# Attention scores on eight array tiles, token reads on two row tiles

## The chip, the cores and the metric

The kernel runs on one core of a Trainium2 chip. The core has a matrix engine (TensorE, PE in the profile; its weight loads are shown as PEld), VectorE (DVE), ScalarE (ACT), GpSimd (POOL) and SyncE (SP, which only issues transfers here). The metric is the device time of one execution in microseconds; lower is better.

## What is computed

Three layers follow one another. The change touches the first and the format in which it hands over.

```python
# attention: B=8, H=8, S=512 tokens, Ns=32 state rows, D=64 a head
scores = scale * x @ state.T              # per batch and head: 512 x 32
a      = softmax(scores, axis=-1)
xread  = a @ state                        # 512 x 64 (reads of the tokens)
scores2 = scale * state @ x.T             # 32 x 512, the same products
sread  = softmax(scores2, axis=-1) @ x    # 32 x 64 (reads of the state)
x = concat([xread, sread], axis=2)        # 4352 tokens of 512, heads side by side
# first expert network: top 1 of 8 experts by cosine logits / tau
out[mask_e] = gate * (relu(x[mask_e] @ w1[e]) @ w2[e])     # 512 -> 1024 -> 512
# second network: h = x @ w_in;  y = (h * clip(h + 3, 0, 6) / 6) @ w_out   # 512 -> 2048 -> 512
```

## The kernel before

**How it is ordered.** All instructions are placed by hand-written planning code (`Sched`, from line 49). Each step is an `op` with a function that emits its instructions, a cost for each engine that may do it, a priority in time, the steps it depends on, and buffers that it takes and gives back (`Ring`, `Hold`). At build time `Sched.run` simulates the engines and emits the steps in the order that the simulation finds. Each engine then runs its own instructions in exactly that order; waits on semaphores are added by the framework. A changed cost, dependency or ring therefore reorders the whole program. The number of buffers of each kind stands in `RG`: four PSUM tiles of two banks in the attention (`ps`), one of each of most intermediate results, and six row buffers (`row`) of which incoming rows may hold five (`rin`).

**The attention, one batch** (`batch`, line 776; steps named `o_...`). The tokens of a batch are loaded for each head (`o_x`, line 489; the first two batches in two halves, `o_xs` and `o_xt`). TensorE transposes pairs of heads (`o_X`, line 529), which puts 2 x 64 channels on the 128 partitions, ScalarE or VectorE copies them to `xT` (`o_Xc`). For each half v of the heads, `o_sc` (line 541) multiplies them with `stT`, the transposed state: for a pair of heads a stationary tile of 128 x 64 with the 32 state rows of one head in its upper left and of the other in its lower right, zeros elsewhere. So a score product contracts over 128 partitions, half of them against zeros, and writes 64 PSUM partitions. VectorE scales the scores to SBUF with a running minimum (`o_scs`). Two softmaxes follow. For the state's reads: exponentials on ScalarE (`o_e2`), transposes (`o_a2`), a copy, and products on column tiles of 128 x 32 (`o_sr`, line 621). For the tokens' reads: transposes (`o_sT`), minimum, subtraction, exponentials, sum, reciprocal, product (`o_rm` to `o_nm`, the last on GpSimd or VectorE), transposes (`o_aT`), a copy (`o_ah`), and for each of four row blocks r the reads (`o_xr`, line 657): for each half g of the heads one product of 128 x 128 with `sd`, the masked state, 264 columns wide. `sd` is made by GpSimd (`o_sd`, line 515); it also carries 8 columns that give each token's expert logits (from `gq`, the state times the expert embeddings). The reads are copied from PSUM to `xr` (`o_xrc`), the logits summed over g (`o_lga` on GpSimd, `o_lg` on VectorE for the last two batches) and `xr` stored to DRAM (`xd`).

**A row of `xd`** has 512 values in four quarters, each with two pieces of 64 values and two partial logits: W = 528 floats, 2112 bytes.

**After the attention** comes the routing (lines 880 to 1120: ranks, slots, indices), then the expert network, which gathers rows of `xd` (`gather` and `parts`, lines 1271 and 1276), rearranges them (`perm`, `blocks`, `bh`, `bl`), multiplies (lines 1412, 1453 and 1515) and stores its outputs (`yt` to `ysd`); interleaved with it the second network reads `ysd` in blocks (`yl`), multiplies (lines 1621 and 1656) and scatters to the output (`yo`). Its weights are converted along the way by ScalarE, VectorE and GpSimd (`convert`, `Conv`; lines 295 to 326), the first ones during the attention. Gathered rows, expert outputs, blocks, final outputs and late conversions share the row buffers.

Of the kernel before, what the change touches and what calls it, by code (L numbers as in the profile page):

```python
# [154 lines left out]
def kernel(  # L155
# [27 lines left out]
    W = DM + 2 * E  # L183
# [32 lines left out]
    def quarters(t, g):  # L216

        v = t.rearrange("p (q g w) -> p g q w", q=4, g=2)[:, g]
        return v[:, :, 0:64].rearrange("p q (i a) -> p q i a", i=2), v[:, :, 64:66]
# [29 lines left out]
    RG = {n: Ring(k) for n, k in dict(  # L249
        ps=4, ax=NAX, xT=NXT, scs=NSC, e2=NE2, e1=NE1, a2=NA2, ah=NAH, xr=NXR, sd=2, sx=1, xs=1, acr=2,  # L250
        m=2, raw=NRAW, w=NW, wraw=NRAW, craw=2, cv=2, cvl=2, gx4=1, gp=2, gx=NGX, gps=6, row=NROW, rin=5, x=1, hx=NHX,
# [130 lines left out]
    SP.dma_start(em, emb)  # L382
# [37 lines left out]

    bmask = one.tile([128, 4], F32, name="bmask")
# [38 lines left out]
    def o_stc(b0, b1, hp):  # L460
        pv = flat(V["st", b0])[:, 0:(b1 - b0) * 256].rearrange("p (u hp n) -> p u hp n", hp=2, n=NS)
        o = stT[64 * hp:64 * hp + 64, b0:b1, :, NS * hp:NS * hp + NS]
        (DVE.tensor_copy if hp else ACT.copy)(o.rearrange("p b u n -> p (b u) n"), pv[64 * hp:64 * hp + 64, :, hp, :])

    def o_gq(b0, b1):
        p = V["gq", b0] = ps("gq_ps")
        for b in range(b0, b1):
            for u in range(4):
                k = (b - b0) * 2 + u // 2
                PE.matmul(p[64 * (u % 2):64 * (u % 2) + 64, 0, k * E:(k + 1) * E],  # L470
                          stT[:, b, u, :], enT[:, u, :], start=True, stop=True)

    def o_gqc(b0, b1):
        ACT.copy(gq[:, b0:b1], V["gq", b0][:, 0, 0:(b1 - b0) * 2 * E].rearrange("p (b g e) -> p b g e", g=2, e=E))
# [14 lines left out]
    def o_x(b, u):  # L489
        if u == 0:  # L490
            V["x", b] = big("xb")[:, 0:R * DM].rearrange("p (r h d) -> p r h d", r=R, h=H)
        SP.dma_start(V["x", b][:, :, u, :], x[b, u].rearrange("(p r) d -> p r d", r=R))
# [8 lines left out]
    def o_xt(e, b, v):  # L501
# [3 lines left out]
        for k in range(2):  # L505
            rs = slice(2 * k, 2 * k + 2)
            {"A": ACT.copy, "D": DVE.tensor_copy, "P": POOL.tensor_copy}[e](
                V["x", b][:, rs, hs, :], V["xs", b][:, hs, rs, :].rearrange("p h r d -> p r h d"))
# [6 lines left out]
    def o_sd(b):  # L515
        t = V["sd", b] = ap2.tile([128, 2, W // 2], F32, tag="sd", name="sd")
        for g in range(2):
            v = t[:, g].rearrange("p (h q w) -> p h q w", h=2, q=2)
            for h in range(2):
                POOL.tensor_tensor(  # L520
                    v[:, h, :, 0:64].rearrange("p q (i a) -> p q i a", i=2),
                    stk[:, b, g, :].rearrange("p (q a) -> p q a", q=2).unsqueeze(2).to_broadcast([128, 2, 2, 32]),
                    bmask.rearrange("p (i h) -> p h i", i=2)[:, h].unsqueeze(1).unsqueeze(3).to_broadcast([128, 2, 2, 32]),
                    op=ALU.mult)
        POOL.tensor_copy(t.rearrange("p g (q w) -> p g q w", q=4)[:, :, :, 64:66],
# [15 lines left out]
    def o_sc(b, v, r0, r1):  # L541
        if (v, r0) == (0, 0):
            V["sc", b] = ps("sc_ps")
        t, k = V["xT", b, v], slice(r0 * 128, r1 * 128)
        for w in range(2):
            PE.matmul(V["sc", b][64 * w:64 * w + 64, v, k], stT[:, b, 2 * v + w, :], t[:, w, k], start=True, stop=True)
# [74 lines left out]
    def o_sr(b):  # L621
        xb, a2 = V.pop(("x", b)), V.pop(("a2", b))
        p = V["sr", b] = ps("sr_ps")
        for g in range(2):
            for r in range(R):
                for h in range(4):
                    PE.matmul(p[NS * h:NS * h + NS, 0, g * D:(g + 1) * D],
                              a2[:, r, (4 * g + h) * NS:(4 * g + h + 1) * NS], xb[:, r, 4 * g + h, :],
                              start=r == 0, stop=r == R - 1)

    def o_sx(b):
        p, r2 = V.pop(("sr", b)), V.pop(("s2", b))
        if b % 4 == 0:
            V["sx", b // 4] = ap1.tile([128, 2, 4, D], F32, tag="sx", name="sx")
# [1240 lines left out]
```

## Time and profile before

| | us |
|---|---|
| median of 3 runs | 1436.18 (1435.46 to 1437.13) |
| the profiled execution | 1427.65 |
| its span, first to last instruction | 1426.0 |
| TensorE busy | 1340.8 (94%) |
| VectorE busy | 867.1 (61%) |
| ScalarE busy | 606.6 (43%) |
| GpSimd busy | 414.7 (29%) |
| mean granted TensorE clock | 0.972 of full |

The profile is one execution, 8.5 us shorter than the median of the timed runs. Times of instructions come from it; busy time is the union of an engine's instructions. Consecutive instructions of an engine overlap a little in the records, so a duration can be some 0.1 us longer than the pace. Matmul ends are modelled. A product of two 32-bit operands shows as two TensorE instructions, a transpose as one.

### The profile page before, as it was taken

The numbers are of one execution on the slowest core, as the hardware profiler recorded it, in microseconds if no ns is written. First come the engines' busy times: TensorE is split into PE (matmuls) and PEld (weight loads), VectorE is DVE, ScalarE is ACT, GpSimd is POOL, SyncE is SP. The second block draws the span as 40 slices with busy tenths as digits, with TensorE's granted clock in tenths as the row PEclk, the third lists the DMA queues.
The fourth block names the chain that finished last, engine by engine and source line by source line (L and its number), as shares of the span: only waits on it lengthen the run. The fifth ranks groups of instructions, "written<-read, shape, count | busy, mean of one in ns | idle before, by whom it ended". The sixth has DMA issues, their size and how long they took to land. (4 is left out here: it accounts for less than half of the span.)

```text
span 1426.0 us, 24825 instructions
## 1 busy us (share of the span) xinstructions
PE 1340.8 (94%) x8912; PEld 1184.8 (83%) x8912; DVE 867.1 (61%) x2037; ACT 606.6 (43%) x1313; POOL 414.7 (29%) x441
## 2 busy tenths in 40 slices
PE   7985797968999999999999999999999999999997
PEld 5764776867789899888989899998989999899996
DVE  6777865777775455545555456777766676434432
ACT  4875635556534333332424333433434444333332
POOL 4333545312343241323223223333334311100000
PEclk9998789997999999999999999999999999999999
DMA  6654346556663243333333334554545544101000
GB/s 163 180 175 165 106 133 201 156 157 205 185 186 113 90 120 112 98 104 91 126 90 120 96 105 125 165 148 141 172 144 163 161 141 141 54 16 31 15 16 15
DMA packets 151761, 175.59 MB, mean 123 GB/s; under 512 B 43784, under 2 KB 116488, under 8 KB 150608
## 3 DMA queue, kind: packets, MB, share of 16 engines
q1 hardware_dynamic: 128544, 121.19, 28.5%
q0 software_dynamic: 12336, 35.99, 8.2%
q10 hardware_dynamic: 10752, 16.78, 3.6%
q8 instruction: 71, 1.16, 0.4%
q14 instruction: 58, 0.48, 0.1%
HBM read 146.09 MB, written 27.82 MB: 122 GB/s over the span
## 5 line engine op out<-in xcount | busy, mean ns | idle before, releaser
L1621 PE MATMUL u_ps<-yh,wih 128*128 128x256 f32 x1088 | 308.3, 283 | 17.0 <-DVE gl L1635 6.9
L1621 PE MATMUL u_ps<-yw,wih 128*128 128x256 f32 x1088 | 307.9, 283 | 0.1
L1621 PE MATMUL u_ps<-yh,wil 128*128 128x256 f32 x1088 | 307.3, 282 | 0.0
L1625 ACT ACTIVATE r<-u_ps,three 128x256 f32<-128x256 f32 x272 | 129.0, 474 | 353.0 <-PE u_ps L1621 350.1
L1628 DVE SCALAR_TENSOR_TENSOR u_ps<-r,u_ps 128x256 f32<-128x256 f32 x272 | 116.5, 428 | 228.9 <-ACT r L1625 224.5
L1621 PEld LDWEIGHTS u_ps<-yh,wih 128*128 128x128 f32 x1088 | 207.9, 191 | 27.3 <-ACT yh L295 6.9
L1656 PE MATMUL o<-woh,gh 128*128 128x512 f32 x544 | 216.5, 398 | 3.0 <-DVE yo L1670 1.8
L1656 PE MATMUL o<-wol,gh 128*128 128x512 f32 x544 | 215.6, 396 | 0.0
L1621 PEld LDWEIGHTS u_ps<-yw,wih 128*128 128x128 f32 x1088 | 207.4, 191 | 8.4 <-DVE yw L1600 0.4
L1656 PE MATMUL o<-woh,gl 128*128 128x512 f32 x544 | 214.3, 394 | 0.0
L1621 PEld LDWEIGHTS u_ps<-yh,wil 128*128 128x128 f32 x1088 | 208.0, 191 | 0.0
L1251 DVE TENSOR_TENSOR wl<-raw,wh 128x512 fp32r<-128x512 f32 x277 | 194.0, 711 | 8.5 <-ACT wh L1248 3.8
L1632 ACT CAST gh<-u_ps 128x256 fp32r<-128x256 f32 x272 | 101.2, 372 | 205.1 <-PE o L1656 170.2
L1515 PE MATMUL y_ps<-wh,hx 128*128 128x512 f32 x512 | 184.8, 397 | 0.0
L1635 DVE TENSOR_TENSOR gl<-u_ps,gh 128x256 fp32r<-128x256 f32 x272 | 114.9, 422 | 110.7 <-ACT gh L1632 110.1
L1251 POOL TENSOR_TENSOR wl<-raw,wh 128x512 fp32r<-128x512 f32 x75 | 103.9, 1385 | 229.1 <-DVE wh L1248 121.7
L1279 POOL DMA_INDIRECT xq<-xd,qidx x128 | 130.2, 1017 | 80.6 <-DVE xt L1332 39.1
L1248 DVE CAST wh<-raw 128x512 fp32r<-128x512 f32 x229 | 102.0, 448 | 65.5 <-DMA raw<-in_moe_w_dram 24.4
L1412 PE MATMUL h_ps<-xt,wh 128*128 128x256 f32 x704 | 136.7, 283 | 1.8 <-DVE wh L1248 1.8
L1675 POOL DMA_INDIRECT out_dram<-yo,ix x34 | 37.0, 1090 | 317.8 <-DVE yo L1670 219.3
L1656 PEld LDWEIGHTS o<-woh,gl 128*128 128x128 f32 x544 | 102.1, 188 | 24.9
L1656 PEld LDWEIGHTS o<-woh,gh 128*128 128x128 f32 x544 | 102.2, 188 | 19.6 <-DVE yo L1670 2.2
(296 smaller groups left out, 2234.0 us busy)
## 6 DMA issues: line engine op xcount, KB each, us to landing
raw<-in_moe_w_dram SPq DMA_DIRECT2D x176, 512.0 KB, 3.9
yl<-ysd SPq DMA_DIRECT2D x136, 64.0 KB, 3.0
xd<-xr SPq DMA_DIRECT2D x8, 1056.0 KB, 5.0
ysd<-yt POOLq DMA_DIRECT2D x32, 256.5 KB, 3.3
xb<-in_x_dram SPq DMA_DIRECT2D x48, 128.0 KB, 3.1
yw<-in_moe_w_out_dram ACTq DMA_DIRECT2D x9, 512.0 KB, 3.5
cv_raw<-in_moe_w_in_dram ACTq DMA_DIRECT2D x8, 512.0 KB, 4.8
yh<-in_moe_w_in_dram ACTq DMA_DIRECT2D x8, 512.0 KB, 5.3
```

The lines of the kernel that those rows point to most:

```text
L1248: copy[e](pc["hi"], box["t"][:, j, :])
L1251: eng[e].tensor_tensor(pc["lo"], box["t"][:, j, :], f32(pc["hi"]), op=ALU.subtract)
L1279: POOL.indirect_dma_start(q[:, j * QW:(j + 1) * QW], None, xd_q, index(qidx[:, j, s:s + 1]))
L1412: PE.matmul(out(f), pc[w][:, (2 * c + f) * 128:(2 * c + f + 1) * 128], u.xt[a][:, 2 * j + c, 256 * hf:256 * hf + 256], start=new and c == ...
L1515: PE.matmul(u.y[i], u.ht[t][:, a, lo + 128 * i:lo + 128 * i + 128], pc[w], start=c == 0 and k == 0, stop=c == KF - 1 and k == 2)
L1621: PE.matmul(p, w, y[:, k, :], start=k == 0 and j == 0, stop=k == KD - 1 and j == 2)
L1625: ACT.activation(q["r"], q["p"], AF.Relu, bias=pool["three"][:, 0:1], scale=unit_i)
L1628: DVE.scalar_tensor_tensor(q["p"], q["r"], 6.0, q["p"], op0=ALU.min, op1=ALU.mult)
L1632: ACT.copy(q["h"], q["p"])
L1635: DVE.tensor_tensor(q["l"], q["p"], f32(q["h"]), op=ALU.subtract)
L1656: PE.matmul(o["o"][a], g[:, a * 128:(a + 1) * 128], w, start=m == 0 and j == 0, stop=m == KFF - 1 and j == 2)
L1675: POOL.indirect_dma_start(out, bass.IndirectOffsetOnAxis(ap=o["ix"][:, a:a + 1], axis=0), box["t"], None)
```

## The change

**Scores.** `stT` becomes a dense tile of 32 columns a pair (no zeros, no clearing); heads u and u + 4 are paired instead of 2u and 2u + 1, so that the tokens and outputs of a batch stand in another order of heads. A score product contracts over 64 partitions and writes 32: eight products a batch, on two row halves (each its own PSUM bank) by four column quarters, in one step that waits for both halves' copies. `o_gq` does the same for the logits.

**Reads of the tokens.** The masked state `sd` has half the columns, and each of four products per row block contracts over 64 partitions and writes 136 columns; the two row halves write different banks. A row now has four pieces of 32 values with two partial logits each in every quarter: W = 544, and each logit is a sum of four parts.

**Planner.** `o_sc` costs 0.1 + 0.00085 n and `o_xr` 0.5 where it was 0.9; the copies `X0c`, `a2c` and `x2c` may go to either engine. Row buffers go from six to five, those for incoming rows from five to four. The rest follows the new format. The diff, cut:

```diff
-    W = DM + 2 * E
+    W = DM + 4 * E
-    NRAW, NW, NROW, NGX = 2, 3, 6, 4
+    NRAW, NW, NROW, NGX = 2, 3, 5, 4
-... row=NROW, rin=5, ...
+... row=NROW, rin=4, ...
-    SP.dma_start(em, emb)
+    for i in range(2):
+        SP.dma_start(em.rearrange("e (u i d) -> e i u d", i=2, u=4)[:, i], emb.rearrange("e (i u d) -> e i u d", i=2, u=4)[:, i])
+    DVE.tensor_tensor(bmask[:, 0:2], bmask[:, 0:2], bmask[:, 2:4], op=ALU.add)
-    stT = one.tile([128, B, 4, 2 * NS], F32, name="stT")
-    DVE.memset(stT[:, 0:1], 0.0)
-    POOL.memset(stT[:, 1:B], 0.0)
+    stT = one.tile([128, B, 4, NS], F32, name="stT")
     def o_gq(b0, b1):
-                PE.matmul(p[64 * (u % 2):64 * (u % 2) + 64, 0, k * E:(k + 1) * E],
-                          stT[:, b, u, :], enT[:, u, :], start=True, stop=True)
+                for g in range(2):
+                    PE.matmul(p[NS * u:NS * u + NS, g, k * E:(k + 1) * E], stT[64 * g:64 * g + 64, b, u, :],
+                              enT[64 * g:64 * g + 64, u, :], start=True, stop=True)
     def o_x(b, u):
-        SP.dma_start(V["x", b][:, :, u, :], ...)
+        SP.dma_start(V["x", b][:, :, 2 * (u % 4) + u // 4, :], ...)
     def o_sd(b):
-            for h in range(2):
-                POOL.tensor_tensor(... 2 x 2 x 32 values, bmask of 4 ...)
+            POOL.tensor_tensor(... 2 x 2 x 32 values, bmask[:, 0:2] ...)
-    def o_sc(b, v, r0, r1):
-        for w in range(2):
-            PE.matmul(V["sc", b][64 * w:64 * w + 64, v, k], stT[:, b, 2 * v + w, :], t[:, w, k], start=True, stop=True)
+    def o_sc(b, r0, r1):
+        for u in range(4):
+            for g in range(2):
+                PE.matmul(V["sc", b][NS * u:NS * u + NS, g, k], stT[64 * g:64 * g + 64, b, u, :],
+                          V["xT", b, u // 2][64 * g:64 * g + 64, u % 2, k], start=True, stop=True)
     def o_xr(b, r):
-            PE.matmul(p[:, g, 0:256 + E], V["ah", b][:, g, r * 128:(r + 1) * 128], V["sd", b][:, g, :], start=True, stop=True)
+            for i in range(2):
+                h = slice(64 * i, 64 * i + 64)
+                PE.matmul(p[:, i, g * QW:(g + 1) * QW], V["ah", b][h, g, r * 128:(r + 1) * 128], V["sd", b][h, g, :],
+                          start=True, stop=True)
     def o_lg(b, r):
-        DVE.tensor_tensor(t, t, p[:, 1], op=ALU.add)
+        for k in range(1, 4):
+            DVE.tensor_tensor(t, t, p[:, k // 2, k % 2], op=ALU.add)
     def o_lga(xr, j, n):
-        POOL.tensor_tensor(lg[...], l[:, :, 0], l[:, :, 1], op=ALU.add)
+        POOL.tensor_tensor(t, l[:, :, 0:2], l[:, :, 2:4], op=ALU.add)
+        POOL.tensor_tensor(lg[...], t[:, :, 0], t[:, :, 1], op=ALU.add)
-        X0c='A', X1c='*', ah='*', nm='P', a2c='A', x0c='*', x1c='*', x2c='A', x3c='*', q1='A')
+        X0c='*', X1c='*', ah='*', nm='P', a2c='*', x0c='*', x1c='*', x2c='*', x3c='*', q1='A')
     def batch(b, t, last):
-                a = do(f"X{v}", o_X, {"T": 0.00085 * n}, xl_[b][4 * v:4 * v + 4], [hX], args=(v, *rr))
+                a = do(f"X{v}", o_X, {"T": 0.00085 * n}, [x_ for i in range(2) for x_ in xl_[b][4 * i + 2 * v:4 * i + 2 * v + 2]], [hX],
+                       args=(v, *rr))
-                f = do(f"c{v}", o_sc, {"T": 0.00086 * n}, [c, *st_ready[b]], ...)
+            f = do("c1", o_sc, {"T": 0.1 + 0.00085 * n}, [*cs_, *st_ready[b]], ...)
-            a = do("xr", o_xr, {"T": 0.9}, deps[r], ...)
+            a = do("xr", o_xr, {"T": 0.5}, deps[r], ...)
```

## Rows read from the trace of the kernel before

**Rows 1.** Busy time by stretch: length, each engine (instructions), clock, DMA share, GB/s

```profile
18.00:104.00 86.00, 80.74 (x966) 60.71 (x965) 63.47 (x138) 65.75 (x111) 28.56 (x46) 1.00 0.59 170
104.00:138.00 34.00, 21.68 (x186) 17.10 (x184) 25.11 (x77) 18.97 (x32) 9.63 (x12) 0.89 0.40 140
...
235.00:400.00 165.00, 136.20 (x796) 119.39 (x796) 117.89 (x261) 92.06 (x189) 50.88 (x51) 0.92 0.61 180
400.00:1426.00 1026.00, 1010.60 (x6455) 909.86 (x6453) 575.72 (x1329) 377.33 (x866) 259.73 (x251) 1.00 0.35 107
```

**Rows 2.** Waits of TensorE, 18 to 104 us: total us, times, longest

```profile
PE sc_ps L546 <- ACT e L566: 1.0, 2, 0.5
```

**Rows 3.** Busy time from 40 to 100 us, columns as in rows 1

```profile
40.00:100.00 60.00, 57.13 (x594) 43.81 (x590) 45.05 (x94) 47.45 (x79) 25.03 (x40) 1.00 0.67 199
```

**Rows 4.** Timeline (start, length, engine, line, operation): scores of batches 2 and 7

```profile
39.37 1.92 PE L546 MATMUL sc_ps<-xT,stT 128*64 128x512 f32 x8
...
97.10 1.52 PE L546 MATMUL sc_ps<-xT,stT 128*64 128x256 f32 x12
```

**Rows 5.** Timeline of one batch: scores of one half, reads, transposes' loads

```profile
50.37 1.08 PE L546 MATMUL sc_ps<-xT,stT 128*64 128x512 f32 x4
...
51.58 3.83 PE L663 MATMUL xr_ps<-sd,ah 128*128 128x264 f32 x16
...
58.59 0.91 PEld L533 LDWEIGHTS xT_ps<-ident,xb 128*128 128x128 f32 x8
```

**Rows 6.** Groups by line, 18 to 131 us: count, busy us, mean ns, idle before

```profile
L666 ACT COPY xr<-xr_ps 128x528 f32<-128x528 f32 x26 | 15.6, 599 | 16.4 <-PE xr_ps L663 11.9 <-issue 4.6
...
L326 POOL TENSOR_TENSOR wil<-cv_m,wih 128x512 fp32r<-128x512 f32 x6 | 7.7, 1279 | 14.1 <-ACT wih L323 14.1
L627 PEld LDWEIGHTS sr_ps<-xb,a 128*32 128x32 f32 x512 | 7.5, 110 | 3.0 <-ACT a L619 1.4 <-DVE e L594 0.8 <-ACT xr L666 0.3
...
L309 DVE SCALAR_TENSOR_TENSOR cv_raw<-cv_raw 128x512 int32<-128x512 int32 x6 | 4.0, 674 | 0.0
```

**Rows 7.** Timeline of the start

```profile
0.87 0.39 SPq L382 DMA_DIRECT2D em<-in_moe_expert_emb_dram  x1
...
1.98 1.59 POOL L429 MEMSET stT<- 128x1792 f32 x1
...
2.77 0.85 DVE L414 TENSOR_SCALAR oi<-orow 128x34 int32<-128x34 int32 x1
...
3.90 0.15 DVE L418 TENSOR_SCALAR oi<-pi 128x1 int32<-128x1 int32 x1
...
6.98 5.22 DVE L441 TENSOR_SCALAR em<-em,ss 8x512 f32<-8x512 f32 x1
```

**Rows 8.** Last batch's token loads, its first transposes, and the loads' landing

```profile
75.92 5.90 SPq L492 DMA_DIRECT2D xb<-in_x_dram  x8
...
86.54 1.04 PE L533 MATMUL xT_ps<-ident,xb 128*128 128x128 f32 x8
...
xb<-in_x_dram SPq DMA_DIRECT2D x48, 128.0 KB, 3.1
```

**Rows 9.** Timeline of the attention's end, and the first gather

```profile
127.05 2.05 PE L663 MATMUL xr_ps<-sd,ah 128*128 128x264 f32 x8 [0.74 <-ACT ah L655]
...
129.97 0.16 DVE L674 TENSOR_TENSOR lg<-lg,xr_ps 128x8 f32<-128x8 f32 x1
...
139.32 1.43 POOL L1273 DMA_INDIRECT xg<-xd,gidx  x1 [13.69 <-DVE cv_raw L309]
```

**Rows 10.** Busy time 160 to 170 us, columns as in rows 1

```profile
160.00:170.00 10.00, 10.00 (x86) 10.00 (x85) 9.65 (x20) 5.64 (x11) 4.18 (x3) 1.00 0.47 151
```

**Rows 11.** Waits, 235 to 400 us, columns as in rows 2

```profile
PE u_ps L1621 <- DVE yt L1539: 4.9, 1, 4.9
...
POOL xg L1273 <- DMA ysd<-yt: 3.9, 2, 3.1
...
ACT yt L1535 <- DMA ysd<-yt: 3.3, 1, 3.3
```

More of the change, by code (lines that the diff above doesn't have):

```diff
@@ L212, with quarters @@
     xd_q = xd.rearrange("t (q w) -> (t q) w", q=4)
-    def quarters(t, g):
-        v = t.rearrange("p (q g w) -> p g q w", q=4, g=2)[:, g]
-        return v[:, :, 0:64].rearrange("p q (i a) -> p q i a", i=2), v[:, :, 64:66]
+    def quarters(t):
+        v = t.rearrange("p (q c w) -> p c q w", q=4, c=4)
+        return v[:, :, :, 0:32], v[:, :, :, 32:34]
     ctx.enter_context(tc.manual_schedule())
@@ L633, in o_sx @@
         if b % 4 == 0:
-            V["sx", b // 4] = ap1.tile([128, 2, 4, D], F32, tag="sx", name="sx")
+            V["sx", b // 4] = ap1.tile([128, 4, 2, D], F32, tag="sx", name="sx")
         sx = V["sx", b // 4]
@@ L638, in o_sx @@
             DVE.tensor_tensor(
-                sx[q:q + NS, :, h, :],
+                sx[q:q + NS, h, :, :],
                 p[NS * h:NS * h + NS, 0, 0:2 * D].rearrange("p (g k) -> p g k", g=2),
@@ L695, in o_q2 @@
         p, t = V["sxp", q], V["sxT", q]
-        for g in range(2):
-            for i in range(2):
-                PE.matmul(p[:, 1, g * 16:g * 16 + E], t[:, 2 * g + i, :], enT[:, 2 * g + i, :],
-                          start=i == 0, stop=i == 1)
+        for c in range(KD):
+            PE.matmul(p[:, 1, c * E:(c + 1) * E], t[:, c, :], enT[:, c, :], start=True, stop=True)
     def o_q3(q):
         xr = V["xrs", q] = ap1.tile([128, 1, W], F32, tag="xrs", name="xrs")
-        for g in range(2):
-            ACT.copy(quarters(xr[:, 0], g)[0],
-                     V["sx", q][:, g].rearrange("p h d -> p (h d)").rearrange("p (i q a) -> p q i a", i=2, q=4))
+        for c in range(KD):
+            ACT.copy(quarters(xr[:, 0])[0][:, c].rearrange("p (h k) a -> p h k a", h=2),
+                     V["sx", q][:, c % 2 * 2:c % 2 * 2 + 2, c // 2].rearrange("p h (k a) -> p h k a", k=2))
     def o_q4(q):
-        for g in range(2):
-            DVE.tensor_copy(quarters(V["xrs", q][:, 0], g)[1],
-                            V["sxp", q][:, 1, g * 16:g * 16 + E].rearrange("p (q i) -> p q i", q=4))
+        DVE.tensor_copy(quarters(V["xrs", q][:, 0])[1],
+                        V["sxp", q][:, 1, 0:KD * E].rearrange("p (c q e) -> p c q e", c=4, q=4))
     PB, P0 = 9.31, 9.54
@@ L1298, in perm @@
             o["q"] = pool["g_p"].tile([128, KD, 128], F32, tag="xp", name="xp")
-            for g in range(2):
-                copy[e](o["q"][:, 2 * g:2 * g + 2, :].rearrange("p i (q a) -> p q i a", q=4), quarters(o["t"], g)[0])
+            copy[e](o["q"].rearrange("p c (q a) -> p c q a", q=4), quarters(o["t"])[0])
         def tr():
```

79 lines of the change are left out of this document (40 added, 39 removed).

## The prediction

> **What bounds the kernel now.** I read the busy time of the engines by stretch first [rows 1]. Up to 104 us, in the attention, TensorE works 80.74 of 86 us. Behind it comes a short stretch to 138 us in which every engine has gaps (the end of the attention and the routing), then the lead of the expert network, from 235 to 400 us a stretch where TensorE is busy 83% of the time, and from 400 us on 98% at full clock. The last kilomicrosecond is therefore bound by TensorE's own work, which the change does not touch: what is won or lost before 400 us simply moves it.
>
> The waits of TensorE in the attention come next [rows 2]: the largest total is 1.0 us, so it runs out of work almost nowhere and is the bound there. The question is how far the others are behind it. Between 40 and 100 us it is busy 57.13 of 60 us, ScalarE 47.45, VectorE 45.05, GpSimd 25.03 [rows 3]. The scores of batch 2 start at 39.37 and those of batch 7 at 97.10 [rows 4]: 57.7 us for five batches, 11.5 us each, of which TensorE has 11.0, ScalarE 9.1 and VectorE 8.7 us. Cutting TensorE alone can bring a batch no lower than about 9.1.
>
> **Part one: the scores.** Before, a batch has two score steps with a column tile for each of two pairs; half of each stationary tile is zeros. A step's four instructions (two passes of two products, 512 columns) take 1.08 us [rows 5]. The reads' sixteen instructions of 264 columns take 3.83 us one after another [rows 5], 0.91 ns a column; four times 512 at that pace would be 1.86 us, so the two column tiles run beside each other already. Afterwards eight products on eight tiles (two row halves by four column quarters) make one step. If all eight run together it takes the same two passes: about 1.1 us a batch instead of 2.16, a saving of 1.08.
>
> **Part two: the reads.** Before, each of four row blocks has two products of 264 columns (four instructions), 3.83 us a batch. Afterwards there are four products of 136 columns, two row tiles at a time: per row block 4 x 136 x 0.91 ns = 0.49 us, 2.0 us a batch, a saving of 1.8. The price unseen in the trace is whether two row tiles load and multiply together. No row shows row tiles. The nearest show column tiles: 512 loads of 32 columns of the state's reads last 110 ns each and cover 7.5 us together [rows 6], so some seven are under way at once. I take full overlap; the other end is a rival below.
>
> The Trainium skill says (TensorE: Matmul & The Clock Gate, Part 3: Packing small matmuls) that a weight load overlaps running products only where its row group differs. These rows show it for column tiles as well, where the page would have none; for row tiles, which the change adds, both point the same way.
>
> **What that is worth.** TensorE's 11.0 us a batch become 8.1. It is then no longer the bound: ScalarE with 9.1 is. The best case is the 95% fill that TensorE has now, 9.6 us a batch; the worst is that the fill of ScalarE rises only from 79% to 82%, 11.1 us, since queues in a fixed order, single buffers and VectorE operations stretched beside GpSimd's, as at the start [rows 7], then take over. I take 90%, because three engines with 8.1 to 9.1 us each hinder one another more than one that leads by two: 10.1 us, 1.4 us a batch. Six batch intervals lie in the stretch: **-8.4 us**, between -2.7 and -12.
>
> **Small parts.** The copies out of PSUM grow from 528 to 544 columns (3% of 0.6 us on ScalarE [rows 6], much the same on VectorE): 0.02 us each, in the noise. A masked state tile costs GpSimd two multiplies a batch rather than four, the sum of logits two adds rather than one: one small operation less, on an engine that works 25 of 60 us [rows 3]. Both halves of a batch must be transposed and copied before its one score step, and the first half needs six loaded heads instead of four. The tightest batch is the last: its eight loads take 5.90 us of issue from 75.92 and land 3.1 us after it, at about 84.9; its first transposes start at 86.54 [rows 8]. That cover of 1.6 us hides the two more issues, 0.7 us each, and I cost it at nothing; without it, it is 1.4 us, once. Each gathered row is 2176 bytes instead of 2112, again nothing.
>
> At the start, GpSimd's clearing of the state tile disappears: 1.59 us, during which a VectorE operation needs 0.85 us where a like one, after it, takes 0.15 [rows 7]. VectorE then reaches the embedding up to 1.3 us sooner; an extra embedding load (0.39 us on SP's queue, ahead of the token and bias loads) eats some of that. The 5.22 us operation that ends the start moves with GpSimd's own sequence: **-1.0 us**, between 0 and -1.3.
>
> At the end, the reads of the last batch come in two halves of 2.05 us, each behind a copy and ahead of the copies that follow [rows 9]; each loses about 1.0. Against it, the logits of the last two batches are now four partial sums: two more VectorE additions of 0.16 us for each row block, of which the last pair lies straight on the way to the routing (the others sit in front of other VectorE work): **-1.6 us** together, between -3 and +1.
>
> **Given back.** A weight conversion runs between the attention's steps, six by 131 us [rows 6], about one for every 18 us. Nine to ten microseconds less attention leave half to one conversion for later, and each has two VectorE operations of 0.67 us [rows 6]. From 160 us on, for some 30 us, VectorE has no room (9.65 of 10 us in the first of them [rows 10]): **+1.4 us**.
>
> The wider rows do not fit six times: the buffers for gathered rows, expert outputs, blocks on their way into the second network, its outputs and late conversions go from six to five, and those for incoming rows from five to four. Already now ScalarE waits 3.3 us for a store of expert outputs before it may write a row, TensorE 4.9 us behind such a VectorE operation, and GpSimd 3.9 us before a gather [rows 11]. Later, above 400 us, gathers lead by tens of microseconds, so only the stretch from 235 to 400 counts, where TensorE is idle 28.8 us [rows 1]. The lower end is 0, the upper half of that idle time again, 14 us; I take **+2.5 us**, nearer the lower end, since half of these waits are off TensorE.
>
> **The sum.** -1.0 - 8.4 - 1.6 + 1.4 + 2.5 = -7.1 us. The profiled execution took 1427.65 us (its span is 1426.0, and 1.65 lie around it) and would take 1420.6. It is 8.5 below the median of the runs shown, 1436.18, from which the prediction is counted: **1429.1 us**. Within this case, the best ends make -16 (1420), the worst +4 (1440).
>
> **Rivals.**
> *Row tiles load one after another.* Eight loads of 128 columns take 0.91 us [rows 5], and a row block of the reads now needs eight instead of four: 0.91 us against 0.96. The reads save 0.2 us a batch, not 1.8; TensorE keeps 9.7 us, a batch at 90% is 10.8, the attention wins 4.7 instead of 8.4: 1432.8 us. For it: nothing in the trace shows two row halves. Against it: the overlap of the column tiles. The Trainium skill states that a load's time is set by its columns, not its rows (TensorE: Matmul & The Clock Gate, LDWEIGHTS); the halved rows then do not help, only the overlap does.
> *The attention is held by the order, not by TensorE.* If the fixed order and single buffers keep a batch at 11.1 us, the sum is -1.0 - 2.7 - 1.6 + 1.4 + 2.5 = -1.4: 1434.8 us, no change that can be measured. For it: ScalarE and VectorE are at 79 and 75%. Against: TensorE waits for hardly anyone now.
> *Slower: one row buffer fewer between 235 and 400 us.* If the waits for a row land on TensorE as the 4.9 us one does, its idle time grows by 14 us: -1.0 - 8.4 - 1.6 + 1.4 + 14 = +4.4, 1440.6 us. It decides from about 10 us more idle time in that stretch. For it: six kinds of rows share the buffers there and late conversions too. Against: the list of waits holds few of them.
>
> **How the numbers follow.** Forecast 0.55, loads in series 0.10, order 0.17, row buffers 0.18. The range 1419 to 1440 takes in the forecast's ends but for a microsecond and half of the slower case. A measurement of this kernel can tell about 0.2% (2.9 us): faster than 1433.3 are nearly all of the forecast and half of the loads in series, 0.60; same 0.22; slower 0.18.
>
> **What the profile will show.** Right: one score step a batch of about 1.1 us; reads of 2.0 us a batch; the attention's batches 10.1 us apart; TensorE's busy share in it down to 80%, ScalarE's up to 90%; the gather of the first expert rows about 11 us earlier than 139 [rows 9]. Wrong: reads near 3.6 us (loads in series), batches still over 11 us, a TensorE clock below full in the attention because it now has gaps, or TensorE idle well above 29 us between the first gathers and the steady part.

## The result and the profile after

The changed kernel takes 1422.93 us (median of four runs, 1420.91 to 1425.92); the kernel before, on the same chip, 1436.66 (1435.46 to 1437.73). The ratio is 0.991, 95% interval 0.9893 to 0.9928: 13.7 us less, where 7.1 less were forecast. The profiled executions are only 2.7 us apart, 1424.93 against 1427.65, because the one shown of before lies at the fast end of that kernel's own spread: in the first experiment below its executions reach from 1428 to 1440 us.

The busy time by stretch, beside [rows 1] (length, each engine with its instructions, clock, DMA share, GB/s), and the stretch from 40 to 100 us, beside [rows 3]:

```profile
18.00:104.00 86.00, 71.26 (x1170) 54.84 (x1162) 63.57 (x136) 66.95 (x116) 28.18 (x41) 0.96 0.60 172
104.00:138.00 34.00, 21.13 (x240) 18.47 (x234) 25.44 (x89) 18.14 (x32) 6.54 (x11) 0.70 0.37 139
...
235.00:400.00 165.00, 140.69 (x814) 125.03 (x815) 118.41 (x259) 93.29 (x190) 62.32 (x59) 0.90 0.60 185
400.00:1423.00 1023.00, 1012.79 (x6443) 913.39 (x6442) 578.92 (x1330) 378.58 (x869) 250.79 (x244) 1.00 0.34 106
...
40.00:100.00 60.00, 49.40 (x800) 38.88 (x800) 48.63 (x102) 50.34 (x91) 23.39 (x36) 1.00 0.67 197
```

TensorE is busy 9.5 us less up to 104 us, and from 40 to 100 us its share falls from 95 to 82%, while ScalarE and VectorE rise to 84 and 81%. Between 104 and 138 us the clock is 0.70 where it was 0.89. The timeline shows what became of the two parts, beside [rows 4, 5, 9] (start, length, engine, line, operation; the scores of batches 0, 1, 6 and 7, one batch's reads at full and one at half clock, the first gather):

```profile
17.38 2.36 PE L549 MATMUL sc_ps<-xT,stT 64*32 64x512 f32 x16
33.42 1.38 PE L549 MATMUL sc_ps<-xT,stT 64*32 64x512 f32 x16
77.67 2.23 PE L669 MATMUL xr_ps<-sd,ah 64*128 64x136 f32 x32 [0.73 <-ACT ah L659]
83.71 1.09 PE L549 MATMUL sc_ps<-xT,stT 64*32 64x512 f32 x16
95.56 1.09 PE L549 MATMUL sc_ps<-xT,stT 64*32 64x256 f32 x32
118.75 4.00 PE L669 MATMUL xr_ps<-sd,ah 64*128 64x136 f32 x32
138.86 1.40 POOL L1283 DMA_INDIRECT xg<-xd,gidx  x1 [12.25 <-DVE three L1199]
```

One score step takes 1.09 us in place of two of 1.08, the reads 2.23 us in place of 3.83. Both parts do in TensorE what they were meant to. And yet the first gather, which ends the attention and the routing, starts at 138.86 where it started at 139.32: **the attention is hardly shorter**, half a microsecond where about 11 were forecast. The gain has to lie elsewhere, and the attention has to lose at other places what it wins here. The experiments had to settle both.

### The profile page after: what moved, and what is told of

It is laid out like the page before. It is cut to its first block, busy times and chain, and to the rows that moved or that the text cites. A ratio compares the mean times of both kernels' runs of the same rounds, so it can differ in the third digit from the quotient of the medians.

```text
span 1423.3 us, 25424 instructions
## 1 busy us (share of the span) xinstructions
PE 1337.1 (94%) x9176; PEld 1189.1 (84%) x9176; DVE 871.8 (61%) x2047; ACT 608.6 (43%) x1318; POOL 410.6 (29%) x430
## 5 line engine op out<-in xcount | busy, mean ns | idle before, releaser
L1420 PE MATMUL h_ps<-xt,wh 128*128 128x256 f32 x704 | 141.0, 289 | 0.0
L1420 PE MATMUL h_ps<-xt,wl 128*128 128x256 f32 x352 | 103.0, 293 | 17.8 <-DVE wl L1261 11.9
```

The source lines that it names most:

```text
L1420: PE.matmul(out(f), pc[w][:, (2 * c + f) * 128:(2 * c + f + 1) * 128], u.xt[a][:, 2 * j + c, 256 * hf:256 * hf + 256], start=new and c == ...
```

## The experiments

Each kernel's timeline gives the start of the scores of batches 0, 1 and 6 and of the first gather; the rest of the span lies behind the gather. Each column comes from one profiled execution, the ratio from all timed ones. Times in us; the ratio is to the runs of before made beside it.

| kernel | scores 0 | 0 to 1 | 1 to 6 | 6 to gather | first gather | behind it | ratio (95%) |
|---|---|---|---|---|---|---|---|
| before, again | 18.27 | 11.5 | 58.8 | 50.8 | 139.4 | 1293.0 | 1.0003 (0.9984 to 1.0023) |
| changed kernel | 17.38 | 16.0 | 50.3 | 55.2 | 138.9 | 1284.4 | 0.9910 (0.9893 to 0.9928) |
| ring alone | 18.27 | 11.5 | 58.9 | 51.0 | 139.6 | 1276.1 | 0.9895 (0.9869 to 0.9921) |
| ring's order, six buffers | 18.27 | 11.5 | 58.9 | 50.9 | 139.5 | 1273.0 | 0.9892 (0.9869 to 0.9915) |
| four input slots alone | 18.27 | 11.5 | 58.8 | 50.9 | 139.5 | 1288.5 | 0.9965 (0.9952 to 0.9978) |
| ring and wide rows | 17.99 | 11.5 | 59.2 | 50.8 | 139.5 | 1282.7 | 0.9925 (0.9905 to 0.9946) |
| scores alone | 17.02 | 12.3 | 53.4 | 51.5 | 134.2 | 1291.2 | 0.9953 (0.9931 to 0.9975) |
| scores and ring | 17.15 | 12.2 | 53.4 | 50.7 | 133.4 | 1277.7 | 0.9848 (0.9825 to 0.9871) |
| the same, scores twice | 17.09 | 13.1 | 57.8 | 52.0 | 140.0 | 1277.9 | 0.9898 (0.9869 to 0.9927) |
| reads (and ring) alone | 18.48 | 11.6 | 56.5 | 50.9 | 137.5 | 1282.4 | 0.9902 (0.9876 to 0.9928) |
| changed, copies as before | 17.38 | 12.6 | 55.2 | 50.8 | 136.0 | 1280.3 | 0.9896 (0.9868 to 0.9924) |
| changed, reads twice | 17.32 | 14.9 | 55.9 | 59.2 | 147.3 | 1282.7 | 0.9987 (0.9970 to 1.0004) |
| changed, one reduction | 17.38 | 14.8 | 50.3 | 53.6 | 136.2 | 1285.6 | 0.9893 (0.9860 to 0.9926) |

### Before, once more

No edit.

> The kernel before, unchanged, beside its own timed runs. The profile of before took 1427.65 us, 8 to 9 us under its three timed runs (1435.46 to 1437.13). Theory 1 (the granted clock): the profile of before was an execution with a higher mean clock (0.972); another profiled execution that takes about 1436 us shows a lower mean clock, near 0.966, and the missing time lies in stretches where TensorE is the bound. Theory 2 (profiling itself): every profiled execution of before is some 8 us under the timed runs, and the comparison of the two profiles (2.7 us) understates nothing that the change did. Ratio 1.00 within 0.2%.

Ten executions took 1427.86 to 1437.30 us, with mean clocks of 0.965 to 0.973, and the profiled one 1434.05 at 0.971. Neither theory stands. The profile is not systematically faster than the timed runs, so the second falls; but 1434 us came at the clock of the fast one too (0.972), so the mean clock is not enough to explain the spread. It has a part in it: over these ten executions and the 19 beside them a lower clock goes with a longer time (correlation -0.49, a quarter of the variance). The profile shown of before was a fast execution of a kernel that spreads over some 10 us; the rest of the spread is open. For times I use ratios, for stretches this second profile of before.

### The ring alone

```diff
-    NRAW, NW, NROW, NGX = 2, 3, 6, 4
+    NRAW, NW, NROW, NGX = 2, 3, 5, 4
...
-row=NROW, rin=5
+row=NROW, rin=4
```

> Before with the smaller ring of row buffers alone (6 to 5, and its input slots 5 to 4); nothing else is changed. The prediction put +2.5 us on it and +14 us as the far end. The trace after the change shows TensorE idle 24.3 us between 235 and 400 where it was 28.8, so the price should be smaller than predicted: theory 1 expects 0 to +2.5 us. Rival: the ring decides when gathers run in the first stage of the experts, and 1 to 2 us of wait for each of some six buffers give +6 to +14 us. A third outcome is a gain: another number of buffers makes another order of the work, worth some us either way.

The third outcome, and larger than anyone expected: this one edit, with the scores and reads of before, takes 1417.35 us beside 1432.76, as much of a gain as the whole change. The first gather does not move; 16.9 us are won behind it. TensorE's waits between 235 and 400 us (total, times, longest), first of before, then with the ring alone:

```profile
PE u_ps L1621 <- ACT yh L1597: 7.1, 1, 7.1
PE u_ps L1621 <- DVE gl L1635: 6.7, 3, 5.7
PE u_ps L1621 <- DVE yt L1539: 5.4, 1, 5.4
PE h_ps L1412 <- DVE wl L1251: 4.2, 6, 1.6
```

```profile
PE h_ps L1412 <- DVE wl L1251: 9.8, 5, 4.3
PE h_ps L1412 <- DVE gates L1360: 6.1, 2, 3.3
...
PE u_ps L1621 <- ACT yh L1597: 2.9, 1, 2.9
```

The stretch itself with the ring alone, beside [rows 1]:

```profile
235.00:400.00 165.00, 142.53 (x838) 127.29 (x838) 122.65 (x268) 96.58 (x199) 62.54 (x59) 0.91 0.61 187
```

In before the dense network's products (`u_ps`) wait 19.2 us for their own operands. With the ring one wait of 2.9 us is left of them; the experts' weights and gates take over part of it, and TensorE is busy 142.53 us of the stretch instead of 136.20 (135.36 in the second profile of before). From 400 to 700 us it is then busy for all 300.00 us instead of 293.04; but the first profile of before has 297.28 there, so that more than half of this second gain lies within the spread of before. The changed kernel shows the new picture as well (its products wait once, 3.7 us, for `yh`).

### The ring's order with six buffers in memory

The planner counts five buffers and four slots, but the memory holds six. Every engine has the same instructions in the same order as with the ring alone.

```diff
 (on the ring alone)
-    ("row", dict(bufs=NROW))
+    ("row", dict(bufs=6))
```

> The order of the work that the planner writes with 5 row buffers and 4 input slots (the same instructions in the same order on every engine as in the run of the ring alone), but with 6 row buffers in memory. Theory 1 (the order): the 15 us that the ring alone brought come from the other order that the planner writes, and not from the number of buffers; this kernel then takes what the ring alone took, ratio 0.989 to 0.991. Theory 2 (fewer buffers themselves hold gathers back and so help): it falls back towards before, ratio 0.995 to 1.000. Theory 3 (fewer buffers still cost some waits): a ratio below 0.988, 1 to 3 us under the ring alone.

The ratio is 0.9892 beside 0.9895, so **the gain is the order that the planner writes, not the number of buffers**. The span with its mean clock, first of the ring alone, then of this kernel:

```profile
core 0: 1415.7 us, clock 0.971
```

```profile
core 0: 1412.5 us, clock 0.975
```

With the sixth buffer this profile is 3.2 us shorter, the median of the runs 1.9 us longer (1419.26 and 1417.35): the buffer itself cannot be told from no change. The converse, the order for six buffers with five in memory, was not tried.

### Four input slots alone

```diff
-row=NROW, rin=5
+row=NROW, rin=4
```

> Before with 6 row buffers and 4 input slots: only the number of rows that may be gathered ahead changes. In before the dense layer's products waited three times for their own rows between 235 and 400 us (7.05, 5.71 and 5.45 us), and with the smaller ring only once (2.9 us). Theory 1 (one buffer more that gathers cannot take lets the rows of the dense layer through): those three waits fall to under 4 us in sum and the ratio is 0.987 to 0.992. Theory 2 (a chance of the order): the waits lie elsewhere, and the ratio is anywhere between 0.99 and 1.005, with at least two waits of over 4 us left in 235 to 400.

Between the theories. The waits of the dense network's products fall from 19.2 to 8.1 us (total, times, longest):

```profile
PE u_ps L1621 <- ACT yh L1597: 4.6, 1, 4.6
...
PE u_ps L1621 <- DVE gl L1635: 3.5, 1, 3.5
...
235.00:400.00 165.00, 132.84 (x746) 113.76 (x744) 114.61 (x252) 88.74 (x180) 46.52 (x50) 0.89 0.57 175
```

and the time falls by 0.35%, a third of the ring's gain. Yet TensorE is busy less in this stretch than before (132.84 us against 135.36), because other products now wait longer. So the waits of the dense network's products go along with a gain but are not shown to be its cause, here or with the ring alone; the order as a whole is. Which order comes out of a ring of a given size cannot be read from its size.

### The ring and wide rows

On the ring alone, rows of 544 elements; scores and reads stay, a second copy of the logits' columns fills the rows. The edit, cut:

```diff
 (on the ring alone)
-    W = DM + 2 * E
+    W = DM + 4 * E
...
-    ... p[:, g, 0:256 + E], V["ah", b] ...
+    ... p[:, g, 0:W // 2], V["ah", b] ...
```

> Before with the smaller ring, and with rows of 544 elements in place of 528 (the 16 more are a second copy of the logits' columns, which nothing reads); scores and reads stay as before, and every engine has the order of the run of the ring alone, with one more copy of 16 columns on GpSimd per batch. In the kernels with the smaller ring and rows of 528 the time from the first gather to the end was 1273 to 1278 us; in those with rows of 544 (reads alone, the changed kernel and its variants) 1280 to 1286 us. Theory 1 (the wider rows cost this themselves, in their conversion and their transfers): first gather at 139.5 to 141 us, 1280 to 1284 us behind it, ratio 0.992 to 0.996. Theory 2 (the order of the kernels with the reads costs it, not the width): 1273 to 1278 us behind the gather, ratio 0.988 to 0.991.

Theory 1. The order is that of the ring alone and the first gather comes at the same time, but 1282.7 us follow it instead of 1276.1, and the runs (1421.48 to 1426.95) lie wholly above those of the ring alone (1416.06 to 1418.74), though the intervals of the two ratios overlap (0.9905 to 0.9946, 0.9869 to 0.9921). Two gathers on the way, first with narrow, then with wide rows:

```profile
447.53 0.98 POOL L1273 DMA_INDIRECT xg<-xd,gidx  x1 [4.22 <-DVE xt L1332]
1105.52 0.98 POOL L1273 DMA_INDIRECT xg<-xd,gidx  x1 [0.30 <-issue]
```

```profile
449.69 0.98 POOL L1273 DMA_INDIRECT xg<-xd,gidx  x1 [4.22 <-DVE xt L1332]
1111.02 1.55 POOL L1273 DMA_INDIRECT xg<-xd,gidx  x1 [0.31 <-issue]
```

2.2 us are lost by 450 us and 3.3 more over the next 660 us, where TensorE is full. The wide rows cost 4.3 us by the ratios and 6.6 by these profiles. What stretches in the long stage stays open: the dense network's products last 282 ns there instead of 281, but so they do in the order with six buffers and narrow rows, which is not slower.

### The scores alone, and with the ring

On before: the score step, the dense state and the pairing of the heads; the reads, the row width and (in the first) the ring stay. The edit, cut:

```diff
+        for u in range(4):
+            for g in range(2):
+                PE.matmul(V["sc", b][NS * u:NS * u + NS, g, k], stT[64 * g:64 * g + 64, b, u, :],
+                          V["xT", b, u // 2][64 * g:64 * g + 64, u % 2, k], start=True, stop=True)
```

> Before with the part of the scores alone: every head's product on a tile of its own, the dense transposed state without its memsets, one step of 16 instructions (1.09 us) in place of two (2.16 us). The columns of the reads, the row width and the ring stay. Theory 1 (TensorE's work sets the attention, the prediction): 1.07 us less per batch and 0.8 us at the start bring the first gather to about 133 to 135 us (it was 139.32) and the time 4 to 6 us down. Theory 2 (the attention is held by the order of the steps and the other engines, not by TensorE): the first gather stays at 138 to 140 us, and the time moves by under 2 us. Theory 3 (a single step that waits for both halves of the transposed tokens costs latency that the halving gives back): batches lie further apart than 11.2 us and the first gather comes later than 139.3.

> The part of the scores and the ring together, without the part of the reads. Theory 1 (the parts add up: 5.2 us earlier gather from the scores, 15 to 17 us behind the gather from the ring): first gather at 134 to 135 us and a ratio of 0.984 to 0.987 (about 1411 to 1414 us where before takes 1433). Theory 2 (every edit makes the planner write another order behind the gather, worth some us by chance): gather at 134 to 135 us again, but the stage behind it anywhere between 1276 and 1293 us, ratio 0.985 to 0.998.

Theory 1 in both. The first gather comes 5.2 us earlier (1.25 of them at the start), the scores of batches 1 to 6 lie 10.7 us apart on average instead of 11.8, about the 1.07 us of TensorE's work that went, and the median falls by 5.4 us. With the ring the two gains add up: ratio 0.9848, gather at 133.4, 1277.7 us behind it. **This kernel, 1412.84 us, is faster than the ring alone and than the changed kernel.**

```profile
40.00:100.00 60.00, 55.60 (x713) 44.36 (x712) 48.33 (x101) 51.21 (x87) 25.76 (x41) 1.00 0.69 206
...
133.41 1.45 POOL L1281 DMA_INDIRECT xg<-xd,gidx  x1 [13.25 <-DVE cv_raw L309]
```

TensorE is still 93% busy from 40 to 100 us.

### The same kernel with every score product issued twice

```diff
+                for _ in range(2):
                     PE.matmul(V["sc", b][NS * u:NS * u + NS, g, k], ...
```

> The kernel with the part of the scores and the ring (first gather at 133.4 us, ratio 0.9848), with every product of the scores issued twice, in the same order on every engine: TensorE's work is back at that of before (1.09 us more per batch, 8.7 us over eight), while the single step and its order stay. Theory 1 (the scores part gained by TensorE's shorter work): the first gather comes at 138 to 142 us and the ratio rises to 0.988 to 0.991. Theory 2 (it gained by the other order that the planner writes): the first gather moves by under 2 us and the ratio stays at 0.984 to 0.987.

Theory 1. A step takes 2.00 us instead of 1.09; batches 1 to 6 take 57.8 instead of 53.4 us, 4.5 us for five times 0.91, and the gather comes 6.6 us later, at 140.0, for eight times 0.91, 7.3 us: nine tenths of the added work is paid. With its work put back, this order reaches the gather when before does (139.4 to 139.6): the scores gained by shorter work, not by another order.

```profile
76.07 2.00 PE L550 MATMUL sc_ps<-xT,stT 64*32 64x512 f32 x32
...
139.97 1.45 POOL L1281 DMA_INDIRECT xg<-xd,gidx  x1 [13.25 <-DVE cv_raw L309]
```

### The reads alone

On before: the reads on two row tiles, `sd` with half the columns, rows of 544 and, as these need the room, the ring. The edit, cut:

```diff
-            PE.matmul(p[:, g, 0:256 + E], V["ah", b][:, g, ...], V["sd", b][:, g, :], start=True, stop=True)
+            for i in range(2):
+                h = slice(64 * i, 64 * i + 64)
+                PE.matmul(p[:, i, g * QW:(g + 1) * QW], V["ah", b][h, g, ...], V["sd", b][h, g, :], ...
```

> Before with the part of the reads alone: two row tiles with half the columns, rows of 544 elements, the ring at 5 and 4; the scores in two steps and the sparse transposed state stay. Theory 1 (TensorE's work sets the attention): 1.6 to 1.75 us less per batch bring the first gather to 128 to 132 us and the time 5 to 9 us down. Theory 2 (held by the order and the other engines): the first gather stays at 138 to 140 us, the granted clock between 100 and 160 us falls below the 0.89 that before had at 104 to 138, and the time moves by under 3 us, unless the stage of the experts gains. If the time falls by over 5 us with the gather at 139, the gain lies behind the gather, and the stages 138 to 235 and 235 to 400 must show it.

Between the theories: the gather comes at 137.5, 2.0 us earlier, and the ratio is that of the ring with wide rows or little better (0.9902 and 0.9925, intervals overlapping). Batches 1 to 6 take 56.5 us, 0.5 us less each, where TensorE has 1.6 less to do: of the reads' shorter work little arrives. The clock from 104 to 138 us is 0.71, as theory 2 said, and the gain behind the gather is the ring's.

### The changed kernel with the copies as before

The change lets the planner choose an engine for three more copies; here they are fixed as in before. (The expectation speaks of four: `X0c`, `a2c`, `x2c`, and `x1c`, which was free already.)

```diff
-        X0c='*', X1c='*', ah='*', nm='P', a2c='*', x0c='*', x1c='*', x2c='*', x3c='*', q1='A')
+        X0c='A', X1c='*', ah='*', nm='P', a2c='A', x0c='*', x1c='*', x2c='A', x3c='*', q1='A')
```

> The changed kernel with the copies on the engines that before gave them (four copies that the change lets the planner choose an engine for are on ScalarE again). With the scores alone, on these fixed engines, the first gather came at 134.2 us; in the changed kernel it comes at 138.9. Theory 1 (the freed copies cost the attention what the smaller columns gained): first gather at 132 to 135 us and 3 to 6 us less than the changed kernel, ratio to before 0.986 to 0.988. Theory 2 (the reads with half the columns let the granted clock fall, and the order in the tail costs the rest): first gather at 137 to 140 us, ratio 0.989 to 0.993. Theory 3 (the freed copies relieve ScalarE): first gather later than 139 us.

The gather comes at 136.0, between the theories; the ratio, 0.9896, cannot be told from the changed kernel's. So **the free copies bring the attention nothing: they go with a gather 2.9 us later** (1.2 of these are a fall of the clock in one execution, see the last experiment). By the table they win 5 us from batch 1 to 6 (50.3 instead of 55.2) and lose 8 before and behind (16.0 and 55.2 instead of 12.6 and 50.8). But this split hangs on the step by which a batch is dated. The reads of the state and of the tokens, batches 1 and 6, first with fixed, then with free copies:

```profile
36.51 1.10 PE L631 MATMUL sr_ps<-xb,a 128*32 128x64 f32 x64
56.18 2.23 PE L669 MATMUL xr_ps<-sd,ah 64*128 64x136 f32 x32 [1.22 <-DVE e L598]
97.53 1.10 PE L631 MATMUL sr_ps<-xb,a 128*32 128x64 f32 x64 [1.11 <-ACT a L623]
113.04 4.00 PE L669 MATMUL xr_ps<-sd,ah 64*128 64x136 f32 x32
```

```profile
41.74 1.10 PE L631 MATMUL sr_ps<-xb,a 128*32 128x64 f32 x64
54.32 1.20 PE L669 MATMUL xr_ps<-sd,ah 64*128 64x136 f32 x16 [1.15 <-DVE rs L606]
102.19 1.94 PE L631 MATMUL sr_ps<-xb,a 128*32 128x64 f32 x64 [1.50 <-DVE e L598]
118.75 4.00 PE L669 MATMUL xr_ps<-sd,ah 64*128 64x136 f32 x32
```

From batch 1 to 6 the state's reads take 61.0 us with fixed copies and 60.5 with free ones, the tokens' reads 56.9 and 64.4. A batch whose scores come late need not be late in its reads; where the order changes, only the sum to the gather can be trusted.

Two places show how the order differs. VectorE's token copies for batch 1, first in this kernel, then in the changed one:

```profile
25.95 1.43 DVE L511 COPY xb<-xs 128x512 f32<-128x512 f32 x4
```

```profile
27.84 1.42 DVE L511 COPY xb<-xs 128x512 f32<-128x512 f32 x4
```

They come 1.9 us later there, and TensorE waits 1.7 us for them. In the last batch the scores need four groups of transposes; in the changed kernel the last group stands behind the state's reads, a softmax transpose and a whole batch of reads in TensorE's queue:

```profile
91.15 2.23 PE L669 MATMUL xr_ps<-sd,ah 64*128 64x136 f32 x32
93.31 0.66 PE L534 MATMUL xT_ps<-ident,xb 128*128 128x128 f32 x4
```

and the last scores come at 95.56. With fixed copies they come at 88.17:

```profile
88.17 1.23 PE L549 MATMUL sc_ps<-xT,stT 64*32 64x256 f32 x32 [0.88 <-ACT xT L540]
```

Only part of these 7.4 us can reach the gather: it follows the last scores by 43.3 us in the changed kernel and by 47.8 with fixed copies.

### The changed kernel with every product of the reads issued twice

```diff
+                for _ in range(2):
                     PE.matmul(p[:, i, g * QW:(g + 1) * QW], V["ah", b][h, g, ...
```

> The changed kernel with every product of the reads issued twice (the second writes the same values over the first), in the same order on every engine. It puts the columns that the change halved back on TensorE: 2.2 us more per batch at the full clock, 17.8 us over eight batches. In the changed kernel the first gather came at 138.9 us and the mean clock was 0.70 between 104 and 138 us. Theory 1 (TensorE has slack in the attention once the columns are halved; the copies and the softmax on ScalarE and VectorE and the order set it): the first gather moves by 0 to 5 us, to 139 to 144, and the time by 0 to 5 us. Theory 2 (TensorE's work still sets the attention): the first gather moves by 12 to 18 us, to 151 to 157, and the ratio to before is above 0.999. Theory 3 (the low clock is what the change lost): with TensorE busier the clock at 104 to 138 us goes above 0.85 and the first gather comes no later than 139.

Between the first two theories, and against the third.

```profile
80.40 4.08 PE L670 MATMUL xr_ps<-sd,ah 64*128 64x136 f32 x64 [0.73 <-ACT ah L659]
...
104.00:138.00 34.00, 24.93 (x362) 22.29 (x362) 23.26 (x70) 18.27 (x34) 8.46 (x12) 0.85 0.29 106
...
147.29 1.40 POOL L1283 DMA_INDIRECT xg<-xd,gidx  x1 [13.06 <-DVE three L1199]
```

A batch's reads take 4.08 us instead of 2.23, a little more than the 3.83 of before. The gather comes 8.4 us later for eight times 1.85, 14.8 us of work: about six tenths of it is paid, where it was nine tenths when TensorE was 93% busy. (Between the scores of batches 1 and 6 lie four batches' reads, 7.4 us more; 5.6 of them are paid.) So the halved columns do win 8.4 us in this order; but with the reads' work put back this order, with its free copies and additions, reaches the gather at 147.3, where the kernel with the scores and the old reads has it at 133.4. The clock from 104 to 138 us rises to 0.85 and the gather still comes later, so theory 3 falls. What the low clock costs by itself was not measured: the reads at 118.75 take 4.00 us instead of 2.23, but the kernel with fixed copies has a clock of 0.66 there and an earlier gather.

### The changed kernel with one reduction for the logits

```diff
-        DVE.tensor_copy(t, p[:, 0, 0])
-        for k in range(1, 4):
-            DVE.tensor_tensor(t, t, p[:, k // 2, k % 2], op=ALU.add)
+        DVE.tensor_reduce(t, p.rearrange("p i g q e -> p q e i g"), axis=AX.XY, op=ALU.add)
```

> The changed kernel with the logits of the last two batches summed by one reduction on VectorE for each of the eight row blocks, where the change has one copy and three additions (four instructions of 0.16 us each, 8 times 0.65 us in sum); all other instructions and their order are unchanged. Theory 1 (these additions stand on the path to the first gather): the gather moves 2 to 3.5 us earlier than 138.9, and the time falls by as much. Theory 2 (they lie beside the reads of the next row block): the gather moves by under 1 us.

The gather comes 2.7 us earlier, but 1.2 of these are won already before batch 1 (14.8 instead of 16.0 us). The order there is the same; the clock is not. Busy time behind the wait for the token copies, first in the changed kernel, then here (columns as in [rows 1]):

```profile
29.00:31.00 2.00, 2.00 (x10) 1.89 (x11) 1.86 (x8) 0.03 (x1) 0.00 (x0) 0.53 0.80 260
```

```profile
29.00:31.00 2.00, 1.70 (x14) 1.35 (x14) 1.86 (x8) 0.85 (x1) 0.03 (x1) 1.00 0.79 240
```

In the profiled execution of the changed kernel the granted clock fell to 1.2 GHz there; here and with the reads twice (14.9 us) it stayed at 2.4, after the same wait of 1.7 us. From the last batch's scores (94.43 here, 95.56 in the changed kernel) to the gather it is 41.8 us instead of 43.3: the additions cost 1.5 us, between the theories. The time does not show it (0.9893 beside 0.9910, intervals overlapping).

```profile
L680 DVE TENSOR_REDUCE lg<-xr_ps x8: 181/191/192, 119.5 to 127.5; 128x8 f32<-128x32 f32 x8
```

## Why the prediction was right, and where it was not

The sign and the range were right, and faster had the largest chance. But the sum was right by accident: two of its terms were wrong by more than the whole forecast, in opposite directions. The range was also narrower than its parts: its worst end, +4, is the forecast with the row buffers alone at their worst; all the worst ends together make +13.7 us, about 1450.

**The bound** was read rightly as far as the scores go: with 1.07 us a batch taken out (the scores alone) the scores come 1.1 us closer on average, and with the work put back in the same order the gather comes 6.6 us later for 7.3 us of work. For the reads it did not hold: 1.6 us a batch taken out (the reads alone) bring 0.5 a batch, and 2.0 us at the gather.

**Both parts' own costs** were right: 1.09 us for a score step (about 1.1 predicted), 2.23 for a batch's reads (2.0). The rival of loads in series, 3.6 us, falls.

The Trainium skill (TensorE: Matmul & The Clock Gate, Part 3: Packing small matmuls) lets a weight load overlap running products where the row group differs, and the reads in 2.23 us agree; its word "only" does not, as the column tiles of [rows 6] show (512 loads of 110 ns each in 7.5 us).

**The start** came 0.9 us earlier against the second profile of before (18.27 to 17.38) and 0.8 against the first; 1.0 was predicted. Its reason held: without the clearing beside it the VectorE operation of 0.85 us [rows 7] takes 0.18.

**The steady batches** hit the number by one count and not by the prediction's own. From batch 1 to 6 the scores are 10.06 us apart on average, where 10.1 was predicted; from batch 2 to 7, the batches from which the 11.5 of before was read, they are 10.6 apart. The single intervals run from 6.9 to 16.0 us, so there is no even pace that could confirm the 10.1, and hitting it was partly luck. The kernel with fixed copies has 11.0 and 10.1 by the same two counts. What the shares do show is that ScalarE and VectorE come in as TensorE falls behind (82, 84 and 81% busy from 40 to 100 us), and that only six tenths of doubled reads are paid.

**The failed step is "What that is worth" together with the small parts.** They turned TensorE's saved work into time, batch by batch, as if the rest of the order stayed, and counted nothing for the free copies, which they did not weigh at all. Start, steady part and end were to bring -11.0 us to the gather and measured -0.6. Step by step, by the first gather: the ring alone has it at 139.6; the scores added, at 133.4; the reads added with fixed copies, at 136.0; the copies freed, at 138.9, of which 1.2 is the clock in that execution. So the scores brought 6.1 us, and the reads, whose saving was the larger half of the forecast, cost 2.6 where they were added to the scores. It is not that their shorter work is worth nothing, since putting it back costs 8.4 us; what came with them costs as much again. Of that, 1.5 us are the additions of the logits (the prediction had two more of 0.16 us for each row block, the last pair on the path). The rest lies in the place of the steps in the new order and in the free copies; which steps, was not tested by themselves. The prediction saw a risk there, "the tightest batch is the last", and costed it at the landing of its loads; the loads were in time but for 0.4 us, and what was late was the place of its transposes in the queue.

**The row buffers** were the other failed step: +2.5 us predicted, between 0 and +14, with a rival built on it. Measured -15 us for the whole edit (ratio 0.9895), and no cost that can be told from none for the missing buffer. The price was worked out as if the order of the work stayed and only waits were added. But the buffers are also what a planner counts, and it wrote another order for everything behind the gather. Of the three waits from which the price was built [rows 11], those of TensorE and ScalarE are gone in the ring's profile, and GpSimd still waits for such a store (2.3 us); longer waits of the same products, 6.9 and 4.4 us for `gl` and `yh`, were in the same view and not in the price. Nothing in the trace said how the next order would be; the bound "below nothing" was excluded without a reason.

**The wide rows** were put at nothing; they cost 4.3 us by the ratios, with an uncertainty as large.

**The conversion given back**, +1.4 us, was not tested: the attention got hardly shorter.

By the ratios the account is: ring -15.1 us, wide rows +4.3, scores, reads and copies together -2.1 (each with some 4 to 5 us of uncertainty). Of the signs that the prediction named, four were of the right kind: the score step, the reads near 2.0 us, the busy shares of TensorE and ScalarE, and TensorE's idle time from 235 to 400 us (24.3, below 29). Three were not: the gather came 0.5 us earlier instead of 11, four of the seven intervals between batches are over 11 us, and the clock is below full after 104 us.

## What to carry to other kernels

Where a planner writes the order, cost every number it reads as a change of its own, and run it alone: here a buffer count brought more than the work that the change was about, and the change's best half with that count (0.9848) beats the whole. When an edit also changes the order, do not read its worth from the distance between two steps of a loop: another step gives another answer. Measure to the end of the stage, and put the saved work back in the new order, which tells shorter work from a changed order. Here an engine that was 93% busy paid nine tenths of such work, at 82% six tenths.

## What the hardware showed that was not expected

In the lead of the changed kernel TensorE runs 34 products of 164 bf16 columns one after another. First its busy time with these products alone (length, PE, PEld, clock, DMA share, GB/s), then the products themselves at either end of it (count, shortest, median and longest in ns, first and last start):

```profile
186.45:188.45 2.00, 2.00 (x7) 1.09 (x8) 1.00 0.43 123
188.45:190.45 2.00, 2.00 (x8) 1.02 (x7) 0.77 0.42 143
190.45:192.45 2.00, 2.00 (x9) 0.95 (x7) 0.50 0.80 298
```

```profile
L1078 PE MATMUL pg_g<-at,bts x9: 472/473/492, 186.5 to 188.8; 128*128 128x164 bf16 x9
...
L1078 PE MATMUL pg_g<-at,bts x12: 473/473/474, 189.7 to 192.9; 128*128 128x164 bf16 x12
...
L1420 PE MATMUL h_g<-x,wh x27: 276/282/289, 179.9 to 186.0; 128*128 128x256 f32 x27
...
L1420 PE MATMUL h_g<-x,wh x8: 415/415/640, 196.2 to 198.8; 128*128 128x256 f32 x8
```

The granted clock falls from 2.4 to 1.2 GHz although the profile shows TensorE without a gap. These products last 473 ns and start 0.29 us apart on either side of the fall, so it is not the clock that sets their pace; what does, and what made the clock fall, is open (the ends of products are modelled, so idle time could be hidden in them). The products behind them pay, with 415 ns where 282 were usual. A busy share of 100% in the profile is thus no sign that the clock stays up.
